# A mixer kernel on one core: single-column normalisation steps and some low parts move from VectorE to GpSimd

## The chip, the core and the metric

The kernel runs on one core of a Trainium2 chip. The engines of the core are TensorE (PE, with PEld for its weight loads), VectorE (DVE), ScalarE (ACT), GpSimd (POOL) and SyncE (SP), whose queue issues all the transfers of this kernel. The metric is the device time of one execution in microseconds, as the median of several runs. Differences of about 0.2% are the least that can be told from no change.

## The reference

The input x has 2048 rows (tokens) of 512 features. It is normalised, goes through a banded attention with 32 heads of 16 features and a window of 256 tokens, and through a two-layer network of width 1792; the two results are multiplied and added to x. Cut to what matters:

```python
def _layernorm(x, axis=-1, eps=1e-5):
    m = jnp.mean(x, axis=axis, keepdims=True)
    v = jnp.var(x, axis=axis, keepdims=True)
    return (x - m) / jnp.sqrt(v + eps)

def _A_ref(x, wqkv, wo):                      # H = 32, Dh = 16, W = 256
    qkv = (x @ wqkv).reshape(B, S, 3, H, Dh).transpose(2, 0, 3, 1, 4)
    q, k, v = qkv[0], qkv[1], qkv[2]
    scores = jnp.einsum("bhqd,bhkd->bhqk", q, k) * (Dh ** -0.5)
    mask = (idx[:, None] - idx[None, :] >= 0) & (idx[:, None] - idx[None, :] < W)
    p = softmax(where(mask, scores, -1e9))
    o = jnp.einsum("bhqk,bhkd->bhqd", p, v)
    return o.transpose(0, 2, 1, 3).reshape(B, S, D) @ wo

def _B_ref(x, w1, b1, w2, b2):
    y = _layernorm(x)
    return gelu(y @ w1 + b1) @ w2 + b2

xn = _layernorm(x)
return x + _A_ref(xn, wqkv, wo) * silu(_B_ref(xn, w1, b1, w2, b2))
```

## The kernel before, in words

**Numbers.** The data is float32. TensorE multiplies in a rounded format (F32R), so every operand is kept as a high part, which is the value rounded by a copy, and a low part, which is the value minus its high part. A product takes three matmuls: high by high, high by low, low by high. Making a low part is one subtraction over a 128 x 512 tile; many of them are made by DVE, some by POOL. [...]

**Tokens and heads.** The 2048 tokens are four chunks of 512, each of four row tiles of 128 tokens. The 32 heads are eight quads of four heads (n = 0 to 7). For a quad and a chunk, `job_qk(n, c)` multiplies the transposed rows (`big`, named xnT in the profile) with the quad's weights (`wqs[n]`, named wqb) into one PSUM bank. Its `finish` writes the high part `hi` (named sh), by ScalarE, and the low part `lo` (named pjr), and sends both through SP's queue into the quad's slot (`slots[n % 2]`, named qk), four sends of the high and two of the low part. For the first quad (n = 0) both parts are made straight from PSUM, the low part by DVE; for later quads ScalarE first copies the bank to SBUF and POOL makes the low part.

**The normalisation.** `layernorm` with `eager` gives for each row tile two functions. `each(i)` takes statistics and aggregates them (named bnA, mvA: mean and variance), adds EPS to the variance (`ve`, one column) and takes the power -1/2 on POOL (`rs`, one column). `end(i)` makes `sh` = -mean x rs (one column, named shift) on DVE and lets ScalarE apply scale and shift to the row tile; row tiles from `n_act` on are applied by DVE from mean and rs instead. The four normalisations of the chunks are named A0 to A3. A0 and A1 have n_act = 3, A2 and A3 have 4.

**Order.** Each engine works through its instructions in the order in which the program issues them, SP from the loads of the third and fourth chunk on too. The prologue normalises and transposes chunk 0, splits the first weights, and normalises chunk 1. Then a loop over t from -16 to 128 issues everything up to the end of the attention. One step t has two halves, `fill_in(t, 0)` and `fill_in(t, 1)`, that hold pieces of projection work; `plan[t]` holds single calls put there with `at(t, ...)`, and `ends[t]` those put there with `behind(t, ...)`; `later(k, fn)` puts a call k half-steps ahead. From t = -12 on a step has also one `max_block`: eight small score matmuls into the PSUM tiles xy and zo, then on DVE one masked copy (named xy) and one maximum (named mt); there is one such pair of PSUM tiles, so a block's matmuls wait for the maximum of the block before. From t = 0 on a step also has two `prob_block`s (scores again, exponential on ScalarE, masks on POOL) and one `pv_step`.

The part of the loop with t < 0 is the prologue of the attention: group c = 1 at t = -12 to -9, c = 2 at -8 to -5, c = 3 at -4 to -1. Each group has `job_qk(0, c)`, two `job_v` of 24 matmuls each, and `job_x(c + 1)`, the transposes of the next chunk with their splits (high part by ScalarE, low part by DVE). The normalisation A2 is issued at the end of t = -13, all four row tiles of it in two pairs; A3 as one pair at the end of t = -9 and one at the end of t = -8 (line 750). The weights of the second quad are split at t = -9 (lines 688 to 691): high part by ScalarE, low part by DVE.

```python
    def pair(l, a):
        return [l[a][0], l[a + 1][0], l[a][1], l[a + 1][1]]
    ln2, ln3 = (layernorm(xs[c], f"A{c}", True, True) for c in (2, 3))
    lns = {-16: [ln1[3][1]], -13: pair(ln2, 0) + pair(ln2, 2), -9: pair(ln3, 0), -8: pair(ln3, 2)}
```

After the loop the network runs chunk by chunk with TensorE; the change does not touch it. The profile puts most instructions down to line 42, that of the helper that records them, so names of tiles tell them apart.

Of the kernel before, what the change touches and what calls it, by code (L numbers as in the profile page):

```python
# [9 lines left out]
F32 = mybir.dt.float32  # L10
# [3 lines left out]
ALU = mybir.AluOpType  # L14
# [4 lines left out]
P = 128  # L19
# [5 lines left out]
EPS = 1e-5  # L25
# [24 lines left out]
def mixer_kernel(ctx, tc, x, wqk, wv, wo, w1, b1, w2, b2, out):  # L50


    nc = SimpleNamespace(**{name: Ordered(tc, name) for name in ("tensor", "vector", "scalar", "gpsimd", "sync")})
# [4 lines left out]
    small = ctx.enter_context(tc.tile_pool(name="small", bufs=3))  # L58
# [9 lines left out]
    def split(dst_hi, dst_lo, src, eng=None):  # L68

        (eng or nc.scalar.copy)(dst_hi, src)  # L70
        nc.vector.tensor_sub(dst_lo, src, dst_hi.bitcast(F32))

    def copy_rows(dst, src):
        nc.sync.dma_start(dst.bitcast(F32), src.bitcast(F32))
# [3 lines left out]
        nc.sync.dma_start(t, src)  # L78
        return t

    def layernorm(ts, name, on_act, eager=False, n_act=4):

        n = len(ts)
        mv = small.tile([P, n, 2], F32, tag="mv", name=f"mv{name}")
        rs = small.tile([P, n], F32, tag="rs", name=f"rs{name}")
        sh = small.tile([P, n], F32, tag="shift", name=f"shift{name}")

        def each(i):  # L90

            stats(i)
            ve = small.tile([P, 1], F32, tag="ve1", name=f"ve{name}_{i}")
            nc.vector.tensor_scalar(ve, mv[:, i, 1:2], EPS, None, op0=ALU.add)
            nc.gpsimd.tensor_tensor(rs[:, i: i + 1], ve, mhalf[:, :1], op=ALU.pow)

        def shift(i):
            nc.vector.scalar_tensor_tensor(sh[:, i: i + 1], mv[:, i, 0:1], -1.0, rs[:, i: i + 1],
                                           op0=ALU.mult, op1=ALU.mult)

        def stats(i):
            st = small.tile([P, 6], F32, tag="bn", name=f"bn{name}_{i}")
            nc.vector.bn_stats(st, ts[i])
            nc.vector.bn_aggr(mv[:, i], st)

        def invert():
            ve = small.tile([P, n], F32, tag="ve", name=f"ve{name}")
            nc.vector.tensor_scalar(ve, mv[:, :, 1], EPS, None, op0=ALU.add)
            nc.gpsimd.tensor_tensor(rs, ve, mhalf[:, :n], op=ALU.pow)

        def shift_all():
            if on_act:
                nc.vector.scalar_tensor_tensor(sh, mv[:, :, 0], -1.0, rs, op0=ALU.mult, op1=ALU.mult)

        def apply(i, on_act=on_act):
            if on_act:
                nc.scalar.activation(ts[i], ts[i], AF.Identity, bias=sh[:, i: i + 1], scale=rs[:, i: i + 1])
            else:
                nc.vector.tensor_scalar(ts[i], ts[i], mv[:, i, 0:1], rs[:, i: i + 1],
                                        op0=ALU.subtract, op1=ALU.mult)  # L120

        def end(i):

            if i < n_act:
                shift(i)
            apply(i, i < n_act)
        if eager:
            return [(lambda i=i: each(i), lambda i=i: end(i)) for i in range(n)]
        return [lambda i=i: stats(i) for i in range(n)] + [invert, shift_all] + [lambda i=i: apply(i) for i in range(n)]
# [5 lines left out]
    def load_x(c, pools, name):  # L135
        return [load(*pools[i % len(pools)], x[512 * c + P * i: 512 * c + P * (i + 1), :], f"{name}_{c}_{i}")
                for i in range(4)]
# [4 lines left out]
    xs = {0: load_x(0, XE, "x")}  # L142
# [9 lines left out]
    wqs = {}  # L152
# [18 lines left out]
    def fill_bank():  # L171

        turn[0] ^= 1
        return fb[turn[0]]
# [55 lines left out]
        raws["v"] = [load(t2, "t2", wv[hf, :, 512 * j: 512 * (j + 1)].rearrange("p (k c) -> p k c", k=2),  # L230
                          f"wvr{hf}_{j}", (P, 2, 256)) for j in range(2)]

    def halves(dst_hi, dst_lo, src, part):

        if part != 1:
            nc.scalar.copy(dst_hi, src)
        if part != 0:
            nc.vector.tensor_sub(dst_lo, src, dst_hi.bitcast(F32))

    def split_wqk(part=None):  # L240
        n, raw = raws["qk"]
        if part != 1:
            wqs[n] = bigp.tile([P, 2, KT, P], F32R, tag=f"wb{n % 2}", name=f"wqb{n}")
        halves(wqs[n][:, 0], wqs[n][:, 1], raw, part)

    def split_wv_part(j):
        split(wva[:, 0, 2 * j: 2 * j + 2], wva[:, 1, 2 * j: 2 * j + 2], raws["v"][j])
# [1 line left out]
    def split_wv(part=None):  # L249
        for j, raw in enumerate(raws["v"]):  # L250
            halves(wva[:, 0, 2 * j: 2 * j + 2], wva[:, 1, 2 * j: 2 * j + 2], raw, part)
# [6 lines left out]
    def later(k, fn):  # L258

        if k == 0:  # L260
            fn()
        else:
            h = 2 * now[0] + now[1] + k
            delayed.setdefault((h // 2, h % 2), []).append(fn)

    def job_qk(n, c):

        box = []
        ops = [(kt, a, b) for kt in range(KT) for a, b in PASSES]
        if not n and c < 2:  # L270
            ops.sort(key=lambda o: o[2])
        sl = slice(512 * c, 512 * (c + 1))

        def mm(i):
            if i == 0:
                box.append(fill_bank() if n or c else xy[:, 0])
            kt, a, b = ops[i]
            nc.tensor.matmul(box[0], wqs[n][:, a, kt], big[:, b, kt, sl],
                             start=(i == 0), stop=(i == len(ops) - 1))

        def send(src, qk, tt):
            copy_rows(slots[n % 2][tt:P:4, qk, :, sl], src[64 * qk: 64 * qk + 64])

        def finish():
            hi = sgp.tile([P, 512], F32R, tag="sh", name=f"sh_{n}_{c}", bufs=2)
            raw = t2.tile([P, 512], F32, tag="t2", name=f"pjr_{n}_{c}")
            lo = raw.bitcast(F32R)
            src = raw if n else box[0]
            if n:
                nc.scalar.copy(raw, box[0])  # L290

            def high():
                nc.scalar.copy(hi, src)
                behind(now[0], send_high)

            def send_high():
                for qk, tt in ((1, 0), (0, 0), (1, 2), (0, 1)):
                    send(hi, qk, tt)

            def low():  # L300
                (nc.gpsimd if n else nc.vector).tensor_tensor(lo, src, hi.bitcast(F32), op=ALU.subtract)
                behind(now[0], send_low)

            def send_low():
                send(lo, 1, 1)
                send(lo, 0, 2)

            later(1 if n else 0, high)
            later(3 if n else 1, low)
        return [(216, mm, i) for i in range(len(ops))], finish  # L310
# [216 lines left out]
    def open_y():  # L527

        t = bigp.tile([P, 4, 512], F32, tag="wa", name="y0")
        mlp["y"] = [t[:, i] for i in range(4)]  # L530
        for i in range(4):
            nc.sync.dma_start(mlp["y"][i], xn_d[i])
        mlp["ln"] = layernorm(mlp["y"], "C0", False)
# [78 lines left out]
    def at(t, fn, *args):  # L612
        plan.setdefault(t, []).append((fn, args))
# [3 lines left out]
    def behind(t, fn, *args):  # L617

        ends.setdefault(t, []).append((fn, args))
# [12 lines left out]
    def transpose0(i):  # L632
        for kt in range(KT):
            nc.tensor.transpose(tr0[kt][:, P * i: P * (i + 1)], xs[0][i][:, P * kt: P * (kt + 1)], ident)
        for _ in range(3 if i < 3 else 0):
            nc.tensor.matmul(zo[:, 0, 0:P], ident, ident, start=True, stop=True)

    ln = layernorm(xs[0], "A0", True, True, 3)
    for i in range(4):
        ln[i][0]()  # L640
# [3 lines left out]
    ln[3][1]()  # L644
    transpose0(3)
    split_wqk(0)
    n, raw = raws["qk"]
    nc.gpsimd.tensor_tensor(wqs[0][:, 1], raw, wqs[0][:, 0].bitcast(F32), op=ALU.subtract)
    for j, raw in enumerate(raws["v"]):
        nc.vector.tensor_copy(wva[:, 0, 2 * j: 2 * j + 2], raw)  # L650
        nc.gpsimd.tensor_tensor(wva[:, 1, 2 * j: 2 * j + 2], raw, wva[:, 0, 2 * j: 2 * j + 2].bitcast(F32),
                                op=ALU.subtract)
    for kt in range(KT):
        split(big[:, 0, kt, 0:512], big[:, 1, kt, 0:512], tr0[kt])
    ln1 = layernorm(xs[1], "A1", True, True, 3)
    for i in range(4):
        ln1[i][0]()
        if i:
# [29 lines left out]
    for n, t in enumerate((-9, 6, 17, 28, 39, 71, 81), 1):  # L688
        at(t - 4, fetch_wqk, n)
        at(t, split_wqk, 0)  # L690
        at(t, split_wqk, 1)
    at(20, fetch_wv, 1)
    at(22, split_wv_part, 0)
    at(26, split_wv_part, 1)
# [51 lines left out]
    def pair(l, a):  # L746
        return [l[a][0], l[a + 1][0], l[a][1], l[a + 1][1]]

    ln2, ln3 = (layernorm(xs[c], f"A{c}", True, True) for c in (2, 3))
    lns = {-16: [ln1[3][1]], -13: pair(ln2, 0) + pair(ln2, 2), -9: pair(ln3, 0), -8: pair(ln3, 2)}  # L750

    def fill_in(t, half):
# [57 lines left out]
    for f in range(6, NF, 2):  # L810
        t = gp.tile([P, 2, 512], F32, tag="ohl", name=f"hr_{f}", bufs=4)
# [35 lines left out]
    for c in range(NCH):  # L847
# [36 lines left out]
        for i in range(NF + 1):  # L884
# [28 lines left out]
            if 9 <= i < 13:  # L913
                raw, rec = wanted
# [74 lines left out]
```

## Time and profile before

| | us |
|---|---|
| median of three runs | 781.3 |
| lowest and highest run | 780.08, 781.41 |
| the profiled execution, its own time | 780.93 |
| span of the profiled execution | 779.3 |
| TensorE busy (matmuls) in the span | 755.6 |
| DVE busy | 486.6 |
| ACT busy | 385.5 |
| POOL busy | 282.4 |

The profile shows one execution. Its span is the time between its first and its last instruction; 1.6 us of the execution's own time lie around it. A line of the page or of a view names the source line, the engine, the operation, the tile written, the tiles read, the shape and the count; the busy time and the mean of one in ns follow, then the time that the engine stood idle just before and what ended it. In the timeline a line starts with the start and the length in microseconds. The chain of waits is followed back from the last instruction: at each point it names the work that the next piece waited for. The granted clock is a share of TensorE's full clock. The prologue with t < 0 lies in the first 70 us of the span.

### The profile page before, as it was taken

To read this page: it belongs to the slowest core of one execution; us is meant where nothing else is said; L and a number is where in the kernel's file an instruction comes from. 1 tells how busy PE (TensorE), PEld (TensorE's weight loads), DVE (VectorE), ACT (ScalarE), POOL (GpSimd) and SP (SyncE) were. 2 spreads that over 40 slices of the span, in tenths; PEclk is the share of its full clock that TensorE was granted. 3 is DMA by queue.
4 is the path that set the end of the run, shared out by engine and by line. 5 is a ranking of instruction groups with operands and counts; after the bars stand their busy time and mean duration, and the time that the engine had idled before them with its cause. 6 is when DMAs were issued, how large, how long until landed. Compare 5 with 4: busy or idle time off the path is not lost.

```text
span 779.3 us, 18595 instructions
## 1 busy us (share of the span) xinstructions
PE 755.6 (97%) x7470; PEld 590.2 (76%) x7470; DVE 486.6 (62%) x787; ACT 385.5 (49%) x636; POOL 282.4 (36%) x567
## 2 busy tenths in 40 slices
PE   9889999999999999999999999999999999999997
PEld 8777676676778887666676677888888888888886
DVE  7886777877767778888873547723464326531243
ACT  6546766867676675777867746321113111221111
POOL 6112666766565554767767600010002000010001
PEclk9999999999999999999999999999999999999999
DMA  7613355635447853555624383610033001210011
GB/s 257 203 44 71 85 130 146 167 95 135 93 110 229 237 190 89 148 134 148 194 77 153 103 280 104 211 47 16 34 108 114 1 27 55 84 52 14 28 54 68
DMA packets 50902, 88.38 MB, mean 113 GB/s; under 512 B 10432, under 2 KB 10688, under 8 KB 50816
## 3 DMA queue, kind: packets, MB, share of 16 engines
q1 hardware_dynamic: 50816, 87.19, 38.5%
q8 instruction: 59, 0.97, 0.5%
q14 instruction: 27, 0.22, 0.1%
HBM read 44.05 MB, written 25.95 MB: 90 GB/s over the span
## 4 chain that ended last, share of the span: by engine, by line
PE 82%; DVE 8%; ACT 4%; issue 2%; POOL 2%; DMA 1%; SPq 0%; DVEq 0%; ACTq 0%; POOLq 0%
PE acc L42 19%; PE h L42 15%; PE fb L42 15%; PE zo L42 12%; PE stb L42 7%; PE s L42 6%; PE xy L42 5%; ACT pt L42 3%; DVE mt L42 2%; DVE xy L42 2%; DVE xnT L42 1%; PE pv L42 1%; POOL pt L42 1%; DVE bnA L42 1%; PE yt L42 1%
## 5 line engine op out<-in xcount | busy, mean ns | idle before, releaser
L42 POOL TENSOR_SCALAR_AFFINE_SELECT pt<-pt 128x256 f32<-128x256 f32 x480 | 196.1, 433 | 156.0 <-ACT pt L42 153.5
L42 ACT ACTIVATE pt<-stb 128x768 f32<-128x768 f32 (+1 forms) x244 | 188.8, 774 | 56.8 <-PE stb L42 48.6
L42 DVE TENSOR_REDUCE mt<-xy 128x4 f32<-128x1024 f32 (+1 forms) x128 | 152.6, 1192 | 4.4
L42 PE MATMUL acc<-w,gh 128*128 128x512 f32 x432 | 133.1, 389 | 0.0
L42 ACT ACTIVATE g<-h,b1s 128x512 f32<-128x512 f32 x44 | 30.4, 690 | 183.6 <-PE h L42 164.5
L42 DVE COPY_PREDICATED xy<-upper,zo 128x512 f32<-128x512 int32 x112 | 77.6, 693 | 67.2 <-PE zo L42 66.5
L42 PE MATMUL fb<-xnT,wqb 64*128 64x512 f32 (+1 forms) x684 | 114.8, 404 | 0.0
L42 PE MATMUL zo<-pt,vt 128*17 128x128 f32 x2880 | 103.7, 275 | 2.3 <-DVE xy L42 1.6
L42 PE MATMUL stb<-qk 64*128 64x384 f32 (+1 forms) x488 | 96.8, 392 | 7.9 <-ACT pt L42 6.4
L42 DVE CAST gh<-g 128x512 fp32r<-128x512 f32 x42 | 17.9, 427 | 128.5 <-PE acc L42 115.8
L42 PEld LDWEIGHTS zo<-pt,vt 128*17 128x17 f32 x2880 | 67.6, 97 | 39.4 <-issue 17.5
L42 PEld LDWEIGHTS acc<-w,gh 128*128 128x128 f32 x432 | 81.1, 188 | 16.9
L42 PE MATMUL h<-xnT 128*128 128x512 f32 x320 | 92.0, 389 | 0.0
L42 PEld LDWEIGHTS stb<-qk 64*128 64x128 f32 x488 | 45.5, 183 | 53.2 <-ACT pt L42 42.6
L42 PE MATMUL acc<-w,gl 128*128 128x512 f32 x216 | 84.3, 390 | 0.8 <-DVE gl L42 0.8
L42 POOL TENSOR_TENSOR xo<-xo,gated 128x512 f32<-128x512 f32 x15 | 19.4, 1292 | 152.6 <-DVE gated L42 146.1
L42 PEld LDWEIGHTS h<-xnT 128*128 128x128 f32 x320 | 60.1, 188 | 12.5
L42 PEld LDWEIGHTS fb<-xnT,wqb 64*128 64x128 f32 (+1 forms) x684 | 63.2, 186 | 6.4 <-issue 0.6
L42 PE MATMUL xy<-qk 64*128 64x256 f32 (+2 forms) x536 | 61.3, 302 | 5.3 <-DVE mt L42 5.2
L42 POOL TENSOR_TENSOR rsC<-veC,mhalf 128x4 f32<-128x4 f32 x6 | 6.6, 1100 | 152.5 <-DVE veC L42 152.5
L42 PEld LDWEIGHTS xy<-qk 64*128 64x128 f32 x536 | 44.1, 185 | 16.2 <-DVE mt L42 10.4
L42 PE MATMUL h<-yh,xnT 128*128 128x512 f32 x160 | 55.7, 389 | 0.0
(135 smaller groups left out, 1006.1 us busy)
## 6 DMA issues: line engine op xcount, KB each, us to landing
qk<-sh SPq DMA_DIRECT2D x128, 128.0 KB
qk<-pjr SPq DMA_DIRECT2D x64, 128.0 KB
oT_d<-oraw SPq DMA_DIRECT2D x32, 256.0 KB
w_d<-in_w_dram SPq DMA_DIRECT2D x14, 512.0 KB
x<-in_x_dram SPq DMA_DIRECT2D x16, 256.0 KB
or<-oT_d SPq DMA_DIRECT2D x16, 256.0 KB
w<-rden_d SPq DMA_DIRECT2D x16, 256.0 KB
xo<-in_x_dram SPq DMA_DIRECT2D x16, 256.0 KB
```

Of the source, the lines that this page charges most:

```text
L42: r = issue(*args, **kwargs)
```

## The change

`layernorm` has a new argument `spare`, set for A1, A2 and A3. With it `each(i)` adds EPS on POOL, and POOL also makes the negated mean (`mm`) and multiplies it with rs into `sh`, behind the power; `end(i)` makes no `sh` on DVE then. For row tile 3 of A1, which DVE applies, POOL makes neither `mm` nor `sh`. The first quad's projections of chunks 1 to 3 are treated as those of later quads: ScalarE copies the PSUM bank to SBUF, makes the high part from the copy, and POOL makes the low part; the half-steps at which these are issued stay as they were. The low part of the second quad's weights (n = 1) is made by POOL. Chunk 0 and A0 stay as they are.

```diff
-    def layernorm(ts, name, on_act, eager=False, n_act=4):
+    def layernorm(ts, name, on_act, eager=False, n_act=4, spare=False):
...
             ve = small.tile([P, 1], F32, tag="ve1", name=f"ve{name}_{i}")
-            nc.vector.tensor_scalar(ve, mv[:, i, 1:2], EPS, None, op0=ALU.add)
+            (nc.gpsimd if spare else nc.vector).tensor_scalar(ve, mv[:, i, 1:2], EPS, None, op0=ALU.add)
             nc.gpsimd.tensor_tensor(rs[:, i: i + 1], ve, mhalf[:, :1], op=ALU.pow)
+            if spare and i < n_act:
+                mm = small.tile([P, 1], F32, tag="mm1", name=f"mm{name}_{i}")
+                nc.gpsimd.tensor_scalar(mm, mv[:, i, 0:1], -1.0, None, op0=ALU.mult)
+                nc.gpsimd.tensor_tensor(sh[:, i: i + 1], mm, rs[:, i: i + 1], op=ALU.mult)
...
         def end(i):
 
-            if i < n_act:
+            if i < n_act and not spare:
                 shift(i)
             apply(i, i < n_act)
...
-    def halves(dst_hi, dst_lo, src, part):
+    def halves(dst_hi, dst_lo, src, part, eng=nc.vector):
 
         if part != 1:
             nc.scalar.copy(dst_hi, src)
         if part != 0:
-            nc.vector.tensor_sub(dst_lo, src, dst_hi.bitcast(F32))
-
-    def split_wqk(part=None):
+            eng.tensor_tensor(dst_lo, src, dst_hi.bitcast(F32), op=ALU.subtract)
+
+    def split_wqk(part=None, eng=nc.vector):
...
-        halves(wqs[n][:, 0], wqs[n][:, 1], raw, part)
+        halves(wqs[n][:, 0], wqs[n][:, 1], raw, part, eng)
...
-            src = raw if n else box[0]
-            if n:
+            src = raw if n or c else box[0]
+            if n or c:
                 nc.scalar.copy(raw, box[0])
...
-                (nc.gpsimd if n else nc.vector).tensor_tensor(lo, src, hi.bitcast(F32), op=ALU.subtract)
+                (nc.gpsimd if n or c else nc.vector).tensor_tensor(lo, src, hi.bitcast(F32), op=ALU.subtract)
...
-    ln1 = layernorm(xs[1], "A1", True, True, 3)
+    ln1 = layernorm(xs[1], "A1", True, True, 3, True)
...
-        at(t, split_wqk, 1)
+        at(t, split_wqk, 1, nc.vector if n > 1 else nc.gpsimd)
...
-    ln2, ln3 = (layernorm(xs[c], f"A{c}", True, True) for c in (2, 3))
+    ln2, ln3 = (layernorm(xs[c], f"A{c}", True, True, spare=True) for c in (2, 3))
```

## The prediction

> **What bounds the kernel now.** I read the page first (busy time, chain), then the chain of waits over the first 82 us, then the timeline and the stretches of the same part, because every edited line is issued there.
>
> ```profile
> PE 755.6 (97%) x7470; PEld 590.2 (76%) x7470; DVE 486.6 (62%) x787; ACT 385.5 (49%) x636; POOL 282.4 (36%) x567
> PE 82%; DVE 8%; ACT 4%; issue 2%; POOL 2%; DMA 1%; SPq 0%; DVEq 0%; ACTq 0%; POOLq 0%
> ```
>
> Over the whole span TensorE is the bound. The prologue differs. Busy time per stretch (length, then PE, PEld, DVE, ACT, POOL, then granted clock, DMA share, GB/s):
>
> ```profile
> 28.65:39.64 10.99, 8.52 (x68) 7.07 (x66) 10.68 (x16) 4.97 (x10) 0.00 (x0) 1.00 0.56 170
> 39.64:50.20 10.56, 8.66 (x54) 7.10 (x54) 8.95 (x26) 4.79 (x8) 2.20 (x4) 0.84 0.29 66
> 50.20:59.20 9.00, 8.97 (x68) 7.45 (x68) 8.53 (x13) 3.95 (x5) 0.00 (x0) 1.00 0.09 18
> 59.20:70.00 10.80, 10.58 (x84) 9.03 (x84) 6.26 (x7) 7.18 (x6) 0.00 (x0) 1.00 0.33 74
> ```
>
> Up to 50 us DVE leads and POOL is nearly free; from 50 us on TensorE is full. So a microsecond taken from the path before 50 us moves everything behind it, and after 50 us DVE time is worth nothing. TensorE's idle time between 28.65 and 50.2 is 2.47 + 1.90 = 4.4 us; no gain from there can exceed that. The chain of waits (start, length) shows the three normalisations of the change:
>
> ```profile
> 13.88 0.61 DVE bnA L42
> ...
> 22.98 0.61 DVE bnA L42
> ...
> 25.07 0.56 POOL rsA L42
> ...
> 28.65 0.68 DVE xy L42
> ...
> 39.64 0.61 DVE bnA L42
> ...
> 42.47 0.10 DVE mh L42
> ...
> 47.70 0.60 DVE pjr L42
> ...
> 50.90 1.03 PE fb L42 x8
> ```
>
> A2 holds DVE from 22.98 to 28.65 (5.67 us for four rows), A3 from 39.64 to 42.47 (2.83 for two) and as long again for the second pair, up to 47.70. In each pair DVE stands still for one power on POOL.
>
> **The unknown price: one row on POOL.** After the change a row is four POOL operations: variance + EPS (ve), power (rs), minus mean (mm), product (sh). The trace has the power, and no tensor_scalar or product of one column. The nearest rows:
>
> ```profile
> L42 POOL TENSOR_SCALAR_AFFINE_SELECT pt<-pt 128x256 f32<-128x256 f32 x480 | 196.1, 433 | 156.0 <-ACT pt L42 153.5 <-DMA w_d<-in_w_dram 1.2
> L42 POOL TENSOR_TENSOR pjr<-pjr,sh 128x512 fp32r<-128x512 f32 x28 | 35.8, 1279 | 0.3 <-ACT sh L42 0.3
> L42 POOL TENSOR_TENSOR rsA<-veA,mhalf 128x1 f32<-128x1 f32 x16 | 8.8, 552 | 28.8 <-DVE veA L42 23.4 <-DVE shiftA L42 5.4
> L42 POOL TENSOR_TENSOR rsC<-veC,mhalf 128x4 f32<-128x4 f32 x6 | 6.6, 1100 | 152.5 <-DVE veC L42 152.5
> L42 POOL TENSOR_SCALAR_AFFINE_SELECT ident<-ident 128x128 f32<-128x128 f32 x1 | 0.3, 295 | 0.1
> L42 POOL MEMSET mhalf<- 128x4 f32 x1 | 0.1, 102 | 0.3 <-POOLq L977 0.3
> ```
>
> Lower end per small operation: 0.10 (the memset). Upper end: 0.55, the power itself; the powers of 1 and 4 columns give 0.18 a column and 0.37 that does not depend on columns, of which the power's own part is unknown. The select of 128 and of 256 columns (0.295, 0.433) leaves 0.16 for no columns, and is the nearest for ve and mm; for the two-input sh I take 0.20. Between operations:
>
> ```profile
> 0.83 0.20 POOL L42 MEMSET ident<- 128x128 f32 x1
> ...
> 1.11 0.29 POOL L42 TENSOR_SCALAR_AFFINE_SELECT ident<-ident 128x128 f32<-128x128 f32 x1
> ...
> 71.34 0.77 POOL L42 TENSOR_SCALAR_AFFINE_SELECT pt<-pt 128x256 f32<-128x256 f32 x2 [23.83 <-ACT pt L42]
> ```
>
> A select that reads the memset before it starts 0.08 after its end; two independent selects take 0.77, 0.10 less than twice the mean of one; I take 0.04 off where neighbours are independent, the half of it rounded down. So a row is 0.16 + 0.08 + 0.55 (rs ready after 0.79) + 0.16 + 0.08 + 0.20 - 2 x 0.04 for the two independent neighbours = **1.15 us**. Ends: 0.93 with every small operation at 0.10 and no gaps, 1.72 with each at 0.37; all at 0.55 (2.3) I hold for very unlikely, since 0.55 contains a power.
>
> [...]
>
> **The change part by part.** Rows of the timeline that the steps use:
>
> ```profile
> 14.52 0.18 DVE L42 BATCH_NORM_AGGREGATE mvA<-bnA 128x2 f32<-128x6 f32 x1
> 14.73 0.15 DVE L42 TENSOR_SCALAR veA<-mvA 128x1 f32<-128x1 f32 x1
> 14.97 0.55 POOL L42 TENSOR_TENSOR rsA<-veA,mhalf 128x1 f32<-128x1 f32 x1 [1.16 <-DVE veA L42]
> 18.13 0.55 POOL L42 TENSOR_TENSOR rsA<-veA,mhalf 128x1 f32<-128x1 f32 x1 [0.52 <-DVE shiftA L42]
> 27.93 1.57 ACT L42 ACTIVATE x<-x,shiftA,rsA 128x512 f32<-128x512 f32 x2 [1.27 <-DVE shiftA L42]
> 29.41 0.56 ACT L42 CAST sh<-fb 128x512 fp32r<-128x512 f32 x1
> 29.87 0.59 ACT L42 COPY vt<-pv 128x512 f32<-128x512 f32 x1
> 31.23 1.07 ACT L42 CAST xnT<-tr 128x512 fp32r<-128x512 f32 x2 [0.76 <-PE tr L42]
> 33.31 2.93 PEld L42 LDWEIGHTS pv<-wva,xnT 128*128 128x128 f32 x24
> 33.77 1.28 DVE L42 TENSOR_TENSOR xnT<-fb,xnT 128x512 fp32r<-128x512 f32 x2
> 36.83 0.68 DVE L42 TENSOR_TENSOR wqb<-wqkr,wqb 128x512 fp32r<-128x512 f32 x1
> 48.46 0.57 ACT L42 COPY vt<-pv 128x512 f32<-128x512 f32 x1
> 50.08 1.31 DVE L42 TENSOR_TENSOR xnT<-tr,xnT 128x512 fp32r<-128x512 f32 x2
> ```
>
> *A1.* The first aggregate ends at 14.70; POOL takes work up 0.09 after its producer (14.88 to 14.97 now), so row 0 starts at 14.79, row 3 at 14.79 + 3 x 1.15 = 18.24, its rs is ready at 19.03. Now it is 18.13 + 0.55 = 18.68. The last row's application on DVE waits for it: **0.35 late**, and so is A2's start (23.33). The ve and shift taken from DVE here buy nothing, because DVE then waits for POOL.
>
> *A2.* DVE needs 4 x 0.82 (statistics 0.61 + 0.02, aggregate 0.19) = 3.3 instead of 5.67, and is free about 2.0 earlier. But ScalarE needs sh: POOL starts at 23.33 + 0.82 + 0.09 = 24.24, four rows end at 28.84, the last application (0.03 to take it up, 0.82) at 29.69; now 29.50. What is queued behind it on ScalarE is next: the new copy of the first-quad projection out of PSUM (between 0.46, the step from sh to vt, and vt's 0.59; I take 0.53), sh, vt, then the transposed rows, which so start at about 31.2 as they do now; the second box of transposes also waits for vt's bank. The four copies end near 33.4, and DVE's last subtraction follows at 34.3 instead of 33.77 + 1.28 = 35.05. So only 0.75 of the 2.0 arrives. TensorE's 24 value matmuls in the same place (33.3 to 36.45 in both) then keep the next score block from starting before 36.5, and at 39.64 the gain is **0.5**.
>
> *A3.* Each pair costs DVE 2 x 0.82 = 1.64 for 2.83, twice 1.2, and the low part of the third chunk goes (0.60): DVE would be 0.5 + 2.4 + 0.6 = 3.5 ahead. ScalarE again sets less: POOL starts the third row at about 44.15 (aggregate after a score block that ends at 43.25), ends the fourth's sh at 46.45, application to 47.3, vt to 47.8, four transposes 0.5, their copy 0.59: 48.9 for DVE's second subtraction, which ends at 49.6 instead of 50.08 + 1.31 = 51.39. Gain there **1.7 to 1.8**.
>
> *The rest.* The weights' low part leaves DVE at 36.83, where DVE next waits for the score block's matmuls: worth nothing; on POOL it takes 1.28, is done by 36 and needed after 59. The fourth chunk's low part lies in the stretch from 59.2, where TensorE is 10.58 of 10.80 busy: nothing. The first-quad sends are later by the copy (0.53) and by the slower subtraction (1.28 for 0.68) and wait in SP's queue in the old order; the second chunk's rows would be issued by 34.3 and are read by the first score block after 39.64, so the cover is some 5 us, less the transfer itself. The third chunk's subtraction is queued behind A3's rows on POOL until 46.5; its rows are read in the stretch after 50.2, by the ninth score block. The copies of the third and fourth chunk cost ScalarE 0.58 each beside idle ScalarE, 0.1 if not.
>
> Sum: -1.7 + 0.1 = **-1.6 us**. The profiled execution had 780.93 us (span 779.3), so 779.3 on its own scale; the runs' median is 0.37 higher, so **779.7** as a median.
>
> **The rivals.**
>
> *POOL rows are dearer (slower).* The place is the same chain; the price decides alone. With small operations at 0.37, a row is 1.72: A1 is 2.3 late, A2's last application ends at 25.25 + 0.91 + 6.88 + 0.85 = 33.9, 4.4 late, DVE's last subtraction at 38.5, 3.4 late, and A3 brings no more back: its fourth row ends at 51.8, the second subtraction at 54.9, 3.5 late. That is 784.8. Between (1.15; -1.7) and (1.72; +3.5) the line crosses zero at a row of 1.34 us, small operations near 0.23 each. For it: the 0.37 left over in the power. Against it: the selects' 0.16.
>
> *POOL rows are cheaper.* At 0.93, A1 is 0.4 early, A2 keeps 1.6, and A3's fourth row is about 3 us ahead: 778.1.
>
> *The clock eats it (same).* The granted clock is lost in one place:
>
> ```profile
> 44.92 0.51 PE L42 MATMUL xy<-qk 64*128 64x256 f32 x4 [1.55 <-DVE mt L42]
> ...
> 45.53 2.29 PE L42 MATMUL pv<-wva,xnT 128*128 128x256 f32 x12
> ```
>
> ```profile
> 46.00:48.00 2.00, 2.00 (x13) 1.99 (x12) 1.33 (x6) 1.02 (x2) 1.06 (x2) 0.59 0.77 173
> 48.00:50.00 2.00, 1.85 (x8) 0.95 (x6) 1.97 (x3) 1.61 (x3) 0.00 (x0) 0.56 0.21 49
> ```
>
> After 1.55 us without a matmul the granted clock is 0.59 and 0.56 over 4 us: (0.41 + 0.44) x 2 = 1.7 us of clock lost, which is 3.4 us at half clock, about from 46.3 on. Now most of that lies beside DVE's chain. In the changed kernel this gap shrinks to some 0.3, but another of about 1.9 opens at 45.5 to 47.3, where TensorE waits for the last application. A 3.4 us stretch at half clock behind it would begin where TensorE is the bound and cost up to 1.7: 781.2. [...]
>
> *It does nothing (same).* The score blocks may wait for rows in DRAM or for TensorE's fixed work instead; 8.5 of 11 us is TensorE's already. 781.
>
> **How the numbers follow.** About 0.2% (1.6 us) is what a measurement of this kernel can tell from no change. Forecast, a row of 1.05 to 1.34 and the clock kept: 0.40, of which 0.22 beyond 1.6 us and 0.18 within; cheaper rows 0.19 (faster); clock or nothing 0.19 (same); dearer rows 0.22 (slower). Faster 0.41, same 0.37, slower 0.22. The range reaches from the cheap row (778.0) to a row of about 1.55 (783.2); the forecast's own is 778.6 to 781.2.
>
> **What the profile after would show.** POOL's groups: twelve ve, eleven mm and eleven sh at 0.16 to 0.2 each, and rows paced 1.15 apart; DVE's aggregates 0.82 apart with no stop for the power; A1's last application near 19.1; ScalarE's last A2 application ending near 29.7, followed by a copy named pjr; DVE's first subtraction of the fourth chunk near 48.3; from 50 us the same pieces, 1.6 earlier. It is wrong if the rows are paced above 1.34, if ve on POOL stops DVE (the power did not: 0.55 beside statistics of 0.68), or if the half-clock stretch falls after 50 us.

## The result, and the profile after

The changed kernel takes **792.32 us** (median of 5 runs, 789.44 to 792.68), beside 781.3 (780.08 to 785.23). The ratio is 1.0118, with a 95% interval of 1.0091 to 1.0144: slower by 9.2 us by the ratio and by 11.0 by the medians (7 to 11 by the interval). The prediction said 779.7 us, range 778.0 to 783.2: wrong in sign and far outside its range. The profiled execution after has 792.23 us (span 790.5), before 780.93 (779.3), a difference of 11.3.

First the page of the kernel after, busy times over the span:

```profile
PE 763.1 (97%) x7470; PEld 593.1 (75%) x7470; DVE 482.0 (61%) x760; ACT 387.6 (49%) x639; POOL 294.6 (37%) x605
```

DVE gave 4.6 us to POOL, which took 12.2. But TensorE, whose work the change does not touch, is 7.5 us longer busy with the same 7470 matmuls; one more stretch at half clock (below) is 1.7 of that. So there are two losses: one in waits and the clock around them, one in the matmuls themselves.

**How the loss is spread.** The start of the same matmul in both timelines (the k-th with its name), after minus before:

| matmul that starts before at (us) | after minus before (us) |
|---|---|
| 14.1 | +0.43 |
| 20.0 | +2.11 |
| 32.0 | +4.51 |
| 48.0 | +2.91 |
| 55.1 to 100 | +4.84 |
| 460 | +5.23 |
| 485 | +5.75 |
| 500 | +6.96 |
| 600 | +8.44 |
| 767 | +11.30 |

Some 4.8 us are lost in the prologue, 0.4 on the way to 460, 1.2 at 485 to 500, and the remaining 4.9 (0.5 before 485, 4.3 behind 500) in the last part, which the change does not edit.

**The prologue.** A2 on POOL in the timeline of the kernel after (start, length):

```profile
29.06 0.21 POOL L42 TENSOR_SCALAR veA<-mvA 128x1 f32<-128x1 f32 x1
29.36 0.57 POOL L42 TENSOR_TENSOR rsA<-veA,mhalf 128x1 f32<-128x1 f32 x1
29.99 0.24 POOL L42 TENSOR_SCALAR mmA<-mvA 128x1 f32<-128x1 f32 x1
30.31 0.19 POOL L42 TENSOR_TENSOR shiftA<-mmA,rsA 128x1 f32<-128x1 f32 x1
30.59 0.21 POOL L42 TENSOR_SCALAR veA<-mvA 128x1 f32<-128x1 f32 x1
```

and its groups (count, then busy time and mean ns of one, then POOL's idle time just before):

```profile
L42 POOL TENSOR_SCALAR mmA<-mvA 128x1 f32<-128x1 f32 x11 | 2.6, 238 | 0.7
L42 POOL TENSOR_SCALAR veA<-mvA 128x1 f32<-128x1 f32 x12 | 2.6, 217 | 12.4 <-DVE mvA L42 11.7
L42 POOL TENSOR_TENSOR shiftA<-mmA,rsA 128x1 f32<-128x1 f32 x11 | 2.1, 191 | 0.9
```

A row takes 30.59 - 29.06 = **1.53 us**: 1.21 of operations (0.21 + 0.57 + 0.24 + 0.19) and 0.32 of gaps. There is a gap of 0.06 to 0.09 behind *each* operation, the independent neighbours too (rs ends at 29.93, mm, which does not read it, starts at 29.99). ScalarE waits for these rows; its timeline after:

```profile
32.07 0.81 ACT L42 ACTIVATE x<-x,shiftA,rsA 128x512 f32<-128x512 f32 x1 [0.72 <-POOL shiftA L42]
32.79 0.56 ACT L42 COPY pjr<-fb 128x512 f32<-128x512 f32 x1
33.38 0.62 ACT L42 CAST sh<-pjr 128x512 fp32r<-128x512 f32 x1
33.91 0.58 ACT L42 COPY vt<-pv 128x512 f32<-128x512 f32 x1
```

A2's last application ends at 32.88; before, it ended at 29.50. The new copy pjr stands between it and vt, and vt's bank is what the next transposes need. TensorE's timeline after, with the idle time and its releaser in brackets:

```profile
32.93 0.33 PE L42 MATMUL tr<-ident,x 128*128 128x128 f32 x1 [1.16 <-ACT x L42]
34.54 1.12 PE L42 MATMUL tr<-ident,x 128*128 128x128 f32 x4 [1.28 <-ACT vt L42]
...
50.95 0.33 PE L42 MATMUL tr<-ident,x 128*128 128x128 f32 x1 [0.67 <-ACT x L42]
52.48 1.13 PE L42 MATMUL tr<-ident,x 128*128 128x128 f32 x5 [1.20 <-ACT x L42]
```

Both chunks' transposes now wait for ScalarE's applications, and these for POOL. The two pauses come with a second price, in the granted clock: 0.83 in each of the two stretches of 10 us that hold them. Stretches of 10 us, first after, then before (length, PE, PEld, DVE, ACT, POOL, then granted clock):

```profile
30.00:40.00 10.00, 7.57 (x52) 6.47 (x51) 6.00 (x8) 5.96 (x10) 4.20 (x8) 0.83 0.65 198
40.00:50.00 10.00, 9.25 (x71) 7.84 (x70) 8.49 (x18) 3.31 (x5) 3.60 (x12) 1.00 0.03 6
50.00:60.00 10.00, 7.99 (x55) 6.92 (x54) 6.66 (x9) 4.40 (x7) 2.48 (x6) 0.83 0.36 83
```

```profile
40.00:50.00 10.00, 8.31 (x54) 6.79 (x50) 8.39 (x24) 4.67 (x7) 2.20 (x4) 0.83 0.29 66
50.00:60.00 10.00, 9.82 (x78) 8.17 (x78) 8.80 (x15) 4.83 (x7) 0.00 (x0) 1.00 0.09 20
```

0.83 over 10 us is 3.4 us at half clock; the traces' clock records have it as 3413 ns at a share of 0.5. Before there is one such stretch, from 46.4 us; after there are two, from 34.1 and 54.6, and the second lies behind 50 us, where TensorE sets the pace.

**The last part.** Three accumulating matmuls in a row of the last part's timeline, before and then after:

```profile
466.38 0.39 PE L42 MATMUL acc<-w,gl 128*128 128x512 f32 x1
...
467.06 0.39 PE L42 MATMUL acc<-w,gl 128*128 128x512 f32 x1
...
467.74 0.39 PE L42 MATMUL acc<-w,gl 128*128 128x512 f32 x1
```

```profile
466.18 0.40 PE L42 MATMUL acc<-w,gl 128*128 128x512 f32 x1
...
466.88 0.40 PE L42 MATMUL acc<-w,gl 128*128 128x512 f32 x1
...
467.59 0.39 PE L42 MATMUL acc<-w,gl 128*128 128x512 f32 x1
```

Between two low-part matmuls lie two others, so three take 0.68 us before and 0.70 to 0.71 after, with no idle time. There are 216 such triples (432 matmuls with gh, two in each): 216 x 0.02 to 0.03 us = 4 to 6 us. The groups in the window 510 to 765 us say the same, before (389 ns) and after (396):

```profile
L42 PE MATMUL acc<-w,gh 128*128 128x512 f32 x336 | 103.5, 389 | 0.0
```

```profile
L42 PE MATMUL acc<-w,gh 128*128 128x512 f32 x312 | 98.3, 396 | 0.0
```

(Each trace holds 432 of them; the window lies at a fixed time and the kernel after reaches it 7 to 11 us later, so the counts differ.) The 1.2 us at 485 to 500 are a wait that stands in both timelines, before and then after:

```profile
486.63 0.50 PE L42 MATMUL acc<-w,gl 128*128 128x512 f32 x1 [0.84 <-DVE gl L42]
```

```profile
493.29 0.50 PE L42 MATMUL acc<-w,gl 128*128 128x512 f32 x1 [1.72 <-DVE gl L42]
```

DVE waits there for a transfer (w from rden_d). In the profiles of the kernels below the shift against before changes by -0.2 to +3.4 us between 485 and 500 us. The three above 3 us (`same_place`, `pad256`, `lows_not_third`) are those with a half-clock stretch there, from 494.7, 491.3 and 489.2 us, behind this wait with 2.3 to 2.6 us; the others, -0.2 to +1.5, have none. Which profiles have it does not follow the edits, so it is read as scatter and profiles are compared up to 440 us.

### The profile page after: what moved, and what is told of

Read it like the earlier page. It is cut to its first block, busy times and chain, and to the rows that moved or that the text cites. A ratio compares the mean times of both kernels' runs of the same rounds, so it can differ in the third digit from the quotient of the medians.

```text
span 790.5 us, 18615 instructions
## 1 busy us (share of the span) xinstructions
PE 763.1 (97%) x7470; PEld 593.1 (75%) x7470; DVE 482.0 (61%) x760; ACT 387.6 (49%) x639; POOL 294.6 (37%) x605
## 4 chain that ended last, share of the span: by engine, by line
PE 79%; DVE 6%; ACT 5%; POOL 3%; DMA 3%; issue 3%; SPq 0%; DVEq 0%; ACTq 0%; POOLq 0%
PE acc L42 18%; PE h L42 15%; PE fb L42 15%; PE zo L42 12%; PE stb L42 7%; PE s L42 6%; PE xy L42 4%; ACT pt L42 3%; PE pv L42 2%; POOL pt L42 2%; DVE xy L42 1%; DVE mt L42 1%; DMA qk<-pjr 1%; DVE xnT L42 1%; DMA w<-rden_d 1%
## 5 line engine op out<-in xcount | busy, mean ns | idle before, releaser
L42 PE MATMUL acc<-w,gh 128*128 128x512 f32 x432 | 136.1, 396 | 0.0
L42 PEld LDWEIGHTS stb<-qk 64*128 64x128 f32 x488 | 45.5, 183 | 53.1 <-ACT pt L42 42.2
L42 PEld LDWEIGHTS xy<-qk 64*128 64x128 f32 x536 | 44.1, 185 | 13.0 <-DVE mt L42 5.6
```

The costliest lines, as they stand in the source:

```text
L42: r = issue(*args, **kwargs)
```

## The experiments

The experiments ran on other chips, on which the kernel before had 783 to 784 us, so medians are compared by ratio, each to before on its own chip. "Ahead" and "behind" are starts of the same matmul against the profile of before.

### Two losses, told apart by placement

What the diff does to TensorE's pace in a part that it does not edit can only be a side effect. One was at hand: the new tag mm1 in the pool `small` has three buffers of 32 bytes, so every tile allocated behind that pool (vt, pt, sh, or, gh, gl, ohl, y, wos) lies 96 bytes higher. `same_place` is the changed kernel with mm in an old tag:

```diff
-                mm = small.tile([P, 1], F32, tag="mm1", name=f"mm{name}_{i}")
+                mm = small.tile([P, 1], F32, tag="ve1", name=f"mm{name}_{i}")
```

> The changed kernel with one edit: the negated mean takes its column from the pool slots of the variance column, so no new slots of three times 32 bytes are made and every later tile (the attention's and the network's) lies at the SBUF addresses of the kernel before; in the changed kernel they lie 96 bytes higher. Theory A (two causes: the prologue arrives 4.8 us late, and from 484 us on the matmuls that load weights from moved tiles are paced 226 to 238 ns instead of 226): the second cause goes, the mean of the acc matmuls is 389 ns again instead of 396, and the time is 786 to 787. Theory B (all of it is the prologue's doing, the late loss being a knock-on of transfers or of the clock): 792, acc matmuls at 396.

`shifted_before` is the kernel before with nothing but the 96 bytes:

```diff
     nc.gpsimd.memset(mhalf, -0.5)
+    nc.gpsimd.memset(small.tile([P, 1], F32, tag="mm1", name="pad"), 0.0)
```

> The kernel before with one edit: three unused columns are reserved in the same pool (one of them is cleared once by GpSimd, 0.1 us beside the first loads), so that all later tiles lie 96 bytes higher as in the changed kernel; every other instruction stays. Theory A: acc matmuls at 396 ns, 5.5 to 6.5 us slower than before, 787 to 788. Theory B: no difference, 781.

Measured: `same_place` 787.61 us, ratio 1.0050 (1.0024 to 1.0075); `shifted_before` 788.33, ratio 1.0063 (1.0039 to 1.0087). The group in the window 510 to 765 us, `same_place` and then `shifted_before`:

```profile
L42 PE MATMUL acc<-w,gh 128*128 128x512 f32 x315 | 97.0, 389 | 0.0
```

```profile
L42 PE MATMUL acc<-w,gh 128*128 128x512 f32 x318 | 100.2, 396 | 0.0
```

So the addresses alone make 396 ns out of 389, without any of the change, and the change without them has 389. `shifted_before` goes from 2.0 behind at 440 us to 7.8 at 767, of which 0.9 at 485 to 500; of the 2.0, 0.7 is a later start and 1.5 the clock (as in `pad256` below), not the addresses. The two ratios add up to 1.0113, beside the change's 1.0118: about half of the loss is placement, half is the prologue.

Which places are slow? `pad64`, `pad128` and `pad256` are `shifted_before` with 2, 4 and 8 buffers instead of 3:

```diff
+    nc.gpsimd.memset(small.tile([P, 1], F32, tag="mm1", name="pad", bufs=8), 0.0)
```

> The kernel before with two unused columns (64 bytes) reserved, so that later tiles lie at a multiple of 64 but not of 128 bytes. If the multiple of 64 counts: acc matmuls at 389 ns. If it is 128, or any move of the tiles against others: 396 ns and 5 us slower.

> The same with four columns (128 bytes). If a multiple of 64 or of 128 counts: acc matmuls at 389 ns. If any move counts: 396 ns.

> The kernel before with 256 bytes of unused columns ahead of the tiles that lie behind the pool small, so that they keep their place modulo 256 bytes. Nothing else is changed. Theory P1 (the matmul pace of the last part goes by the place of its operands modulo 256 bytes): the matmuls acc<-w,gh take 389 ns as before, starts 226 ns apart, and the kernel takes the time of before, 781 to 784 us. Theory P2 (any move against the tiles ahead of the pool, such as the weights w, does it): 396 ns, starts 226 to 240 ns apart, and 786 to 789 us.

One time each: 788.61, 786.1 and 785.72 us. The group in the same window, for 64, 128 and 256 bytes:

```profile
L42 PE MATMUL acc<-w,gh 128*128 128x512 f32 x319 | 100.4, 395 | 0.0
```

```profile
L42 PE MATMUL acc<-w,gh 128*128 128x512 f32 x326 | 102.5, 396 | 0.0
```

```profile
L42 PE MATMUL acc<-w,gh 128*128 128x512 f32 x326 | 100.4, 389 | 0.0
```

Moves of 64, 96 and 128 bytes cost 6 to 7 ns a matmul, a move of 256 nothing: theory P1 as far as five placements can tell (0 and 256 against the three between). The starts of the same matmuls say it too: from 500 to 767 us the four profiles with moved tiles (after, `shifted_before`, `pad64`, `pad128`) lose 4.3 to 4.5 us, `pad256` and all with the old placement 0.0. Which operand it is, gh, gl or the output's neighbours, wasn't tried. `pad256`'s one time misses P1's 781 to 784 and is 1.8 above the 783.92 of before on its chip, and its profile says where: 1.5 us between 48 and 55 us (the clock, below) and 3.2 at 485 to 500.

### Which part of the change loses in the prologue

`norms_only` has the old placement and only the normalisations' edits; `lows_only` the old placement and only the low parts and weights.

> The changed kernel with the old placement, and with the low parts of the first quad and of the second quad's weights back as before; only the normalisations' columns are on GpSimd. Theory A1 (the row of 1.53 us on GpSimd carries the prologue's loss): A2's last application on ScalarE still ends 3 us later than before, and the time is 784 to 786. Theory A2 (the extra copies out of PSUM on ScalarE, behind the late applications, carry it): 781 to 782.

> The changed kernel with the old placement and the normalisations as before; only the low parts of the first quad's chunks 1 to 3 and of the second quad's weights are on GpSimd. Theory A1: the copies on ScalarE are mostly hidden and DVE gains little, 780 to 782. Theory A2: 783 to 785.

Measured: `norms_only` 785.83, ratio 1.0031 (1.0017 to 1.0046); `lows_only` 786.67, ratio 1.0036 (1.0020 to 1.0052). `norms_only` is 1.59 behind at 20 us, 3.33 at 32, 1.77 at 48 and 3.68 from 55 on. Its clock in the stretch behind 50 us:

```profile
50.00:60.00 10.00, 8.66 (x58) 7.55 (x57) 7.19 (x11) 4.24 (x8) 0.35 (x2) 0.83 0.28 63
```

So the dear rows cost 1.8 us, and the half-clock stretch behind 50 us another 1.9. All three profiles with the dear rows (after, `same_place`, `norms_only`) have two half-clock stretches in the prologue, from 33 to 34 and from 53 to 55 us; no other profile has more than one. The whole change's 4.84 is this, 0.52 of a later start of the prologue in its profile (+0.43 against -0.09 at 14 us, which varies from -0.56 to +0.69 among the profiles here), and the copy pjr on ScalarE (0.56): 3.68 + 0.52 + 0.56 = 4.76. `same_place`, the whole change at the old placement, bears the copy out: from its own start it loses 4.34 up to 55 us, `norms_only` 3.77.

For `lows_only` the theories fell: its loss is larger than they gave it, and its timeline shows an origin that neither named. (The profile is that of its quickest run, 783.67; what the other runs, 784.25 to 787.36, lost beyond it is not in a trace.)

```profile
47.52 1.26 POOL L42 TENSOR_TENSOR pjr<-pjr,sh 128x512 fp32r<-128x512 f32 x1
47.58 1.21 DVE L42 SCALAR_TENSOR_TENSOR shiftA<-mvA,rsA 128x1 f32<-128x1 f32 x1 [0.60 <-POOL rsA L42]
...
49.69 0.33 PE L42 MATMUL tr<-ident,x 128*128 128x128 f32 x1 [1.48 <-ACT x L42]
```

A shift of one column takes 0.15 us elsewhere; here it takes 1.21, as long as POOL's subtraction beside it lasts: it starts 0.06 behind it (47.58 and 47.52) and ends 0.01 behind it (48.79 and 48.78). A3's last application and the transposes wait for it. Why it is long beside the subtraction no trace shows. `lows_not_third` leaves the third chunk's low part on DVE, so that POOL does nothing beside that shift:

```diff
-            src = raw if n or c else box[0]
-            if n or c:
+            src = raw if n or c in (1, 3) else box[0]
+            if n or c in (1, 3):
...
-                (nc.gpsimd if n or c else nc.vector).tensor_tensor(lo, src, hi.bitcast(F32), op=ALU.subtract)
+                (nc.gpsimd if n or c in (1, 3) else nc.vector).tensor_tensor(lo, src, hi.bitcast(F32), op=ALU.subtract)
```

> lows_only with the third chunk's low part of the first quad back on DVE, straight from PSUM; the second and fourth chunk's and the weights' stay on GpSimd. In lows_only a shift of one column on DVE took 1.21 us instead of 0.15 while that subtraction of 1.26 us ran on GpSimd, in the middle of A3. Theory C (that one instruction, blocked by the subtraction, carries the loss of lows_only): no shift above 0.2 us, and the time is within 0.2% of before (782 to 784). Theory A2 (the copies out of PSUM on ScalarE carry it, two of three stay): 785 to 786.

Measured: 782.87 us, ratio 1.0008 (0.9991 to 1.0024), and its group of shifts:

```profile
L42 DVE SCALAR_TENSOR_TENSOR shiftA<-mvA,rsA 128x1 f32<-128x1 f32 x14 | 2.1, 152 | 2.4 <-POOL rsA L42 2.4
```

The loss of `lows_only` is gone. The edit takes that chunk's copy on ScalarE away along with the subtraction, so the run alone does not tell the two apart; the timeline above does for 0.8 us. In the whole change that long shift cannot occur, since there no shift of A2 or A3 is on DVE; so it bears on `lows_only` and not on the change. In the profile it is 0.8 of the 2.07 us that `lows_only` is behind; the other 1.2 come between 50 and 52 us, in a half-clock stretch, such as `pad256` below has without any change:

```profile
50.00:60.00 10.00, 9.86 (x69) 8.52 (x69) 8.26 (x14) 4.70 (x7) 0.00 (x0) 0.83 0.12 28
```

### The row and the clock

If the length of POOL's row decides, a short row must win. `short_row` (old placement, no low parts moved) leaves the variance sum on DVE and makes power and shift on POOL, the shift in one operation:

```diff
+            if spare and i < n_act:
+                nc.gpsimd.tensor_scalar(sh[:, i: i + 1], mv[:, i, 0:1], rs[:, i: i + 1], -1.0, op0=ALU.mult, op1=ALU.mult)
```

> The kernel before with the normalisations A1 to A3 alone changed, and less of them on GpSimd than in the changed kernel: the variance column stays on DVE (which then waits for nothing), GpSimd makes the power and, as one operation with two factors (rs and -1), the shift. No new slots, low parts as before. Theory A1 (the length of a GpSimd row decides): a row is 0.57 + 0.08 + 0.24 + 0.06 = 0.95 us instead of 1.53, near DVE's own 0.90 a row; A2's last application on ScalarE ends near 28.8 instead of 29.5 (before) and 32.5 to 32.9 (changed), and the time is 0.5 to 1.5 below before. Theory A3 (any normalisation whose shift comes from GpSimd loses, because ScalarE hands its work on later or because TensorE's idle stretches trip the clock a second time): 785 to 786, as norms_only.

Measured: 782.67 us, ratio 0.9998 (0.9983 to 1.0012): no difference, so neither theory's time came. The row did what it should. POOL's group, and A2's last application:

```profile
L42 POOL TENSOR_SCALAR shiftA<-mvA,rsA 128x1 f32<-128x1 f32 x11 | 2.9, 265 | 1.1
```

```profile
27.91 0.81 ACT L42 ACTIVATE x<-x,shiftA,rsA 128x512 f32<-128x512 f32 x1 [0.26 <-POOL shiftA L42]
```

The application ends at 28.72 instead of 29.50, and the matmuls are 1.23 us ahead at 32 us and 1.73 at 50. From 55 us on they are 0.19 ahead. What took the 1.5 us stands in the stretches:

```profile
40.00:50.00 10.00, 7.85 (x58) 6.50 (x58) 8.91 (x20) 5.32 (x8) 3.24 (x8) 0.96 0.36 82
50.00:60.00 10.00, 9.99 (x68) 8.50 (x67) 7.60 (x12) 4.53 (x6) 0.00 (x0) 0.87 0.03 5
```

The half-clock stretch now lies mostly behind 50 us. That can happen without any change, too. The prologue of `pad256` is that of before but for one memset at its start, and in its profile the stretch fell later:

```profile
40.00:50.00 10.00, 7.47 (x54) 6.07 (x54) 8.39 (x24) 4.62 (x7) 2.20 (x4) 1.00 0.26 59
50.00:60.00 10.00, 9.51 (x66) 8.43 (x66) 8.11 (x14) 4.16 (x5) 0.00 (x0) 0.83 0.12 27
```

`pad256` lost 1.5 us there (0.33 behind at 41 us, 1.84 at 55). Five profiles have this prologue, the tiles' places apart: before and `pad128`, with the stretch from 46.4 and 45.5 us, lose nothing by it, `pad64`, `pad256` and `shifted_before`, with the stretch from 50.9 to 51.7, lose 1.5 each.

In the traces' clock records the first half-clock stretch lasts 3413 ns wherever there is one in the prologue, and its start lies 8, 12 or 13 times 3413 ns behind the first record of the full clock (27.3 us after, 41.0 us before). With the time from that record on cut into pieces of 3413 ns, the piece ahead of a fall holds 1.3 us (`short_row`, 0.40 and 0.75 among them) to 2.0 us (`lows_only`) of pauses. Before's pause of 1.55 us lies in one piece and the clock falls at its end, at 46.4; in `pad256` the end of a piece cuts the same pause at 44.1 us, and the clock falls one piece later, at 50.9, behind three more pauses. A piece of `lows_only` with 1.4 us of pauses (43.5 to 46.9) is not followed by a fall. So what makes the clock fall is not shown.

To separate chain and clock, `short_row_warm` fills TensorE's pauses before the fourth chunk's third and fourth transpose with nine transposes into a corner of zo that nobody reads, and `before_warm` gives the kernel before the same nine and ten more in its pause at 43.4 us, with nothing moved:

```diff
+            for _ in range({2: 3, 3: 6}.get(k, 0) if c == 3 else 0):
+                nc.tensor.transpose(zo[:, 1, 384:512], upper, ident)
             nc.tensor.transpose(box[kt][:, P * i: P * (i + 1)], xs[c][i][:, P * kt: P * (kt + 1)], ident)
...
+        for _ in range(10 if (n, qb) == (0, 5) else 0):
+            nc.tensor.transpose(zo[:, 1, 384:512], upper, ident)
```

(The last two lines are those of `before_warm` alone.)

> short_row (the variance sum stays on VectorE, GpSimd makes the power and the shift in one operation, first part of the prologue otherwise as before, placement of before) with nine idle transposes into an unused corner of zo, three ahead of the third and six ahead of the fourth transpose of the fourth chunk, so that TensorE does not stand still for 0.40 and 0.75 us while it waits for the last two applications. Theory C1 (short_row's 2.3 us at 48 us were lost to the half-clock stretch that those pauses set off just where TensorE becomes the bound): no half-clock stretch between 40 and 60 us, matmuls 1.5 to 2.3 us ahead of before from 50 us on, 780.7 to 781.9 us where before has 783.0. Theory C2 (the gain ends at 50 us whatever the clock, since TensorE's own work or the rows in DRAM come next): 782.4 to 783.5 us, no difference from before; the half-clock stretch may go without the time following.

> The kernel before with idle transposes only: ten into the unused corner of zo ahead of the sixth score block, where TensorE stands still for 1.55 us, and the nine of short_row_warm ahead of the third and fourth transpose of the fourth chunk. Nothing is moved between engines. Theory C1 (the stretch at half clock at 46 to 50 us lies beside VectorE's chain, which ends at 51.4 us either way, and so costs the kernel before nothing; what short_row_warm gained came from the shorter chain together with the kept clock): no half-clock stretch in the first 60 us, matmuls from 58 us on within 0.4 us of before, ratio within 0.1% of 1. Theory C3 (the idle transposes help by themselves, whatever VectorE does): 1.3 to 1.8 us below before, ratio near 0.998, as short_row_warm has.

Measured: `short_row_warm` 781.68 us, ratio 0.9978 (0.9964 to 0.9992); `before_warm` 783.31, ratio 1.0004 (0.9994 to 1.0015). `short_row_warm` and then `before_warm` in the stretch behind 50 us:

```profile
50.00:60.00 10.00, 9.62 (x74) 8.06 (x73) 8.77 (x13) 5.36 (x6) 0.00 (x0) 1.00 0.07 16
```

```profile
50.00:60.00 10.00, 9.62 (x76) 7.90 (x74) 8.62 (x13) 4.61 (x7) 0.00 (x0) 1.00 0.07 16
```

Neither has a half-clock stretch. `short_row_warm` keeps 1.55 us of lead at 55 us and 1.25 at 440 (0.51 of it is an earlier start). `before_warm`, with the same clock, has no gain: its ratio is as theory C1 has it, but its profile is 0.7 behind from 55 us on, beyond C1's 0.4. And it is no clean control, since the idle transposes did not only fill the pauses, they waited for DVE's reading of zo first. This is the one ahead of the third transpose, in `short_row_warm` and then in `before_warm`, with DVE's next subtraction in the latter:

```profile
46.51 0.52 PE L42 MATMUL zo<-ident,upper 128*128 128x128 f32 x3 [0.93 <-DVE xy L42]
```

```profile
48.74 0.55 PE L42 MATMUL zo<-ident,upper 128*128 128x128 f32 x3 [1.47 <-DVE xy L42]
...
50.81 1.29 DVE L42 TENSOR_TENSOR xnT<-tr,xnT 128x512 fp32r<-128x512 f32 x2 [0.87 <-ACT xnT L42]
```

In before that subtraction starts at 50.08 without a wait. So in `before_warm` not DVE's chain but the real transposes behind the idle ones set the end of the prologue, 0.9 us later counted from its own start, and a gain from the kept clock may be hidden by that. That the short chain and the kept clock are needed together is therefore not shown.

The runs' mean granted clocks say more. One half-clock stretch takes 0.002 off the mean (half of 3.4 us in 780), so a run at 0.999 or 1.000 has none. Such runs take 780.75 to 782.02 in `short_row` (three of 12, mean 781.2), 779.17 to 782.78 in `short_row_warm` (eight of 12, mean 781.1), and 781.3 to 782.0 in the kernel before on the chips of the experiments (five of 84, mean 781.6). The runs at 0.997 or less have a mean of 783.7 in `short_row` (six) and 784.0 before (37). So a kept clock goes with some 2.5 us in either kernel, and with the idle transposes it is kept more often, not always; where it is kept, the short chain is some 0.4 us ahead of before by these means, over several chips and few runs. The ratios of `short_row` and `short_row_warm` differ by 0.2%, and their intervals overlap.

`short_row_warm_lows` adds the weights' low part and those of the second and fourth chunk on POOL:

```diff
-        at(t, split_wqk, 1)
+        at(t, split_wqk, 1, nc.vector if n > 1 else nc.gpsimd)
```

(and the lines of `lows_not_third`).

> short_row_warm, and besides the low part of the second quad's weights and those of the first quad's second and fourth chunks by GpSimd as in the change; the third chunk's stays on VectorE. Theory L1 (these three were put where VectorE waits anyway or TensorE is the bound, so they are worth nothing): the time of short_row_warm within 0.7 us. Theory L2 (they bring the 0.6 us by which lows_not_third was ahead up to 440 us): 0.4 to 0.8 us below short_row_warm. Theory L3 (the second chunk's copy out of PSUM delays ScalarE in the part that now sets the pace, A2's end): 0.3 to 0.8 us above short_row_warm.

Measured: 780.37 us, ratio 0.9958 (0.9943 to 0.9973), the fastest kernel of this case: 3.3 us below before on its chip. By the medians it lies 1.3 us below `short_row_warm`, more than any theory gave; in the profiles the two have the same lead at 440 us (1.22 and 1.25), but one started 0.65 late and the other 0.51 early at 14 us, so that counted from their starts they are 1.87 and 0.74 ahead. The runs at a mean clock of 0.999 or more agree (six with a mean of 780.1, beside 781.1). That points to about 1 us for the three low parts; the intervals overlap, so it is not shown.

## Why the prediction was wrong

**The row's price failed, in its gaps more than in its operations.** Predicted 1.15 us; measured 1.53. The operations are 1.21 for 1.07 predicted (0.16 + 0.55 + 0.16 + 0.20). The gaps are 0.32 for 0.08: the step "two independent selects take 0.77, 0.10 less than twice the mean" took overlap between independent neighbours from two long selects and gave it to short ones, which have gaps instead. (The ends of the price were also mislabelled: 0.93 holds the net gaps of 0.08; with none it is 0.85.) The break-even was right in form: the rival "POOL rows are dearer" draws a line through (1.15; -1.7) and (1.72; +3.5), which at 1.53 gives +1.8; `norms_only` is 1.77 behind at 48 us and 2.17 at 50.

**A1** was to be 0.35 late; it is 1.68 (2.11 at 20 us less the 0.43 that it starts late). The predicted 0.35 and 0.38 more for each of the three rows ahead of the last make 1.49.

**A2**'s last application was to end at 29.69; it ends at 32.88. The same formula with 1.53 gives 32.4 (24.24 + 3 x 0.38 for A1's rows, + 4 x 1.53 + 0.85), and 0.43 of later start. That ScalarE and not DVE would set what follows was right, but the copy pjr, counted as no later than the old start of the transposed rows, lies in the chain once the application is late, with its 0.56.

**A3**'s gain of 1.7 to 1.8 became a loss of 3.3 at 50 us: its rows too are paced by POOL, and TensorE's 1.20 us wait for x.

**The clock** was a rival of "same" and priced nearly right (up to 1.7; measured 1.9 in `norms_only` and 1.5 in `short_row`). The error was to let it stand alone. A stretch behind 50 us comes with the dear rows (all three profiles), with the cheap ones (`short_row`), and in three of five profiles of the unchanged prologue; its price had to be added to every case and a gain of 1.6 kept only if no stretch fell behind 50 us.

**"The rest" at about nothing** (0.1) held within the change but for the copy's 0.56; alone, the third chunk's low part cost 0.8 us, as a shift on DVE took 1.21 us instead of 0.15 beside POOL's subtraction. The prediction missed that: its test, a power of 0.55 us beside DVE's statistics of 0.68, was on another DVE instruction and another POOL operation.

**Missing altogether: the tiles' places.** The diff's new tag moved every later tile by 96 bytes, which costs 0.5 us before 485 and 4.3 behind 500, the largest single term. No step of the prediction asked what an allocation does. With the right row (+3.5 on 779.7), clock (1.9), copy (0.56), start (0.43), drift to 460 (0.4, unexplained), placement (4.9) and the stretch 485 to 500 (1.2) the sum is 792.6, beside 792.32. Its terms are read off the profiles, so this shows that they are complete, and is no test of them.

## What to carry to other kernels

Moving single-column work to GpSimd pays only if the row fits under the engine that waits for it: here every operation but the power costs 0.19 to 0.27 us and a gap of 0.06 to 0.10, and two of them a row gained some 1.5 us ahead of the bound where four lost 1.8; behind the bound nothing of the 1.5 was left in the time of the twelve runs. A new small tile is not free either: it moves all tiles behind it (by 96 bytes here, which cost 4.3 us behind 500 us), so give it an existing tag or, as far as one run here can tell, 256 bytes, and compare the matmuls' mean in an untouched part before reading anything else. Where a gain ends at an engine whose granted clock falls for a while, as TensorE's does here (0.83 over 10 us beside pauses, 1.00 with the pauses filled), look at which side of the change of bound the slow stretch lies, and compare runs of the same clock. Filling the pause is not free: the filler can wait for the same engine and hold up the work behind it, as it did in `before_warm`.

## What was not expected of the hardware

- TensorE's accumulating matmuls take 389 ns with the moved tiles at 0 or 256 bytes from the place before, and 395 to 396 at 64, 96 or 128: 4.3 to 4.5 us from 500 to 767 us.
- A 128 x 1 shift on DVE took 1.21 us instead of 0.15 beside a 1.26 us subtraction on POOL (`lows_only`).
- The same prologue, but for a memset, had its 3.4 us at half clock from 45.5 and 46.4 us in two profiles (`pad128`, before) and from 50.9 to 51.7 in three (`pad64`, `pad256`, `shifted_before`), worth 1.5 us.
- The normalisation's short operations on POOL have a gap of 0.06 to 0.10 us between them, also where one does not need the other's result (0.06 between rs and mm).
